# Wider sums, another order of x units, a later operand sum and an earlier transpose in a fused attention and mixer kernel

## The chip, the cores and the metric

The kernel runs on one core of a Trainium2 chip. The metric is the device time of one execution, in microseconds (us); the median of three runs stands for a kernel. One further execution is recorded by the profiler, and all durations below come from that one.

Engines are named as in the profile: PE is TensorE's matmuls and PEld its weight loads, DVE is VectorE, ACT is ScalarE, POOL is GpSimd, and SP is the queue that issues most DMA transfers. [...]

## The reference

Two stages follow each other, over 8 batches of 576 rows. The first is linear attention with 8 heads of 64 columns:

```
q_p, k_p = phi(q), phi(k)      # relu, times a cosine and a sine of the row: 64 -> 128 features
kv  = k_p^T v ;  z = sum of k_p over the rows
x   = (q_p kv) / (q_p z + 1e-06)
```

The second is a low-rank mixer over rows and a two-layer network over the 512 columns:

```
u   = x + ((x^T U) V)^T                 # U: 576 x 32, V: 32 x 576
out = u + relu(u w1) w2                 # w1: 512 x 2048, w2: 2048 x 512
```

Inputs and output are float32; the matmuls run in bfloat16.

## The kernel before

The 576 rows of a batch are held as four chunks of 128 rows (c = 0 to 3) and a tail of 64 rows (c = 4); two batches' tails share one tile. The order on each engine is the order in which the program is written: nothing is rescheduled. The program is a list of **slots**, each a piece of PE work that is large (one `g1` unit of four 128x512 matmuls into `g_ps`, or a quarter of an output tile, `g2_part`, four matmuls into `o_ps`, or an eighth part of a Strassen-like product, `half_part`, eight 128x256 matmuls into `h_ps`). Between the slots hang smaller pieces, keyed by slot number: `at(j, ...)` for batch 1, `attention_plan` with the table `PLAN` for batches 2 to 7, and `put` for operand sums and stores. Each piece runs behind the slot with its number. So attention of the next batch is woven into the network of the one before, and PE always has a slot to go on with.

The parts that the change touches:

- **Batch 0's start** (`first_chain`, from L1119). PE sums k over the rows: for each chunk and head one matmul with a column of ones (`v_tl[:, 0, D:E]`) as its moving operand, into one column of `z_ps` (L1207), with one 128x512 matmul on zeros per chunk for nothing but PE's activity (L1212). ACT copies the 8 columns to `z_sb` (L126). `den_mm` (L1053) then forms the denominators `d_ps`: two matmuls write the constant 1e-06, in two parts, and 20 matmuls with one column of `z_sb` each add to it; DVE takes the reciprocal (L1130, L1141). `z_ps`, `d_ps` and the later x units use the one two-bank tile X, so each waits until the one before it is emptied.
- **Batch 1's x units** (slots 15 to 24). `kv_unit` twice (bank T, emptied by DVE), then one x unit per chunk. `x_unit` (L418) writes eight matmuls into X; DVE adds 1e-06 to the denominators, takes the reciprocal and multiplies (L408, L409, L428). `x_two` (L1268) writes four heads to bank T and four to a bank called `side`, with a reciprocal each, and for batch 1 ACT multiplies all eight heads, one 128x64 product at a time (L1278). The order is unit 0 (`x_two`) and 4 behind slot 18, 1 and 2 (`x_two`) behind 20, 3 behind 21. `A_unit` behind slot 23 (bank T) needs all five, `u_mm` and four `u_add` follow behind 24, and DMA transposes turn u into `uT` (L514), which batch 1's first `g1` reads at slot 32.
- **Operand sums** (`hid_sum`, L818). Each half of a Strassen-like product needs four sums over `hid`. The fourth is issued inside `half_part`, right behind the second product, ahead of whatever hangs behind that slot. Its reader is the product with number 3.
- **Batch 5's q transposes** (`PLAN[5]`). After the q features, three DMA transposes on SP bring q into the layout that the x units read: the tail (`q_tlT`, L392) and two halves (`q_pT`, L387). The table's third tuple gives their slots relative to 127: the tail at 113, the halves at 120 and 122. Between them SP issues two `uT` transposes of batch 4 (slots 117 and 119) and the query load of batch 6 (slot 119). SP issues strictly in order, and `q_pT` has one buffer, free when batch 4's last x unit (slot 112) has read it.

Of the kernel before, what the change touches and what calls it, by code (L numbers as in the profile page):

```python
# [17 lines left out]
def kernel(  # L18
# [22 lines left out]
    NJ = DH // P  # L41
    NPAIR = B // 2
    TS = 64
    EPS = (9.98377799987793e-07, 1.622538547962904e-09, 1.0)

    def tail(b):
# [171 lines left out]
    V_.memset(v_ext[:, 0:4, :, D:E], 1.0)  # L218
    V_.memset(q_tlT, 0.0)
    V_.memset(x_tl, 0.0)  # L220
    eps = pool.tile([1, 2 * P + 20], BF16, tag="S2", bufs=2, name="eps")
    for cs, part in zip((slice(0, P), slice(P, 2 * P), slice(2 * P, None)), EPS):
        V_.memset(eps[:, cs], part)

    def keep_warm(n, tag, bufs, short=0, cols=P):
# [103 lines left out]

    def k_of(b, c, h):  # L330
        return k_p[b][:, c, h, :] if c < 4 else k_tl[:, h, :]

    z_sb = const.tile([P, H], BF16)

    def kv_unit(b, hg, tag, bufs, eng=None, n=E):
        if b not in kv_sb:
# [481 lines left out]
        eng.tensor_tensor(out=o, in0=x, in1=y, op=op)  # L818

    ring, turn = ["o0", "o1"], [0]  # L820
    halves = {}

    def bank(i):
# [20 lines left out]
    def half_part(b, n, k, form):  # L844


        c2 = n + 2
        i = ORDER[form][k]
        if k == 0:
            halves[b, n] = {  # L850
                "o": [
                    pool.tile([P, DM], FP32, tag="o_sb", bufs=8, name="o_sb") for _ in range(2)
                ]
            }
            if form == "alone":
                halves[b, n]["s"] = pool.tile([P, DM], FP32, tag="o_sb", bufs=8, name="s_sb")
        w = halves[b, n]
        s1, s2 = hid_s.get((b, n, 1)), hid_s.get((b, n, 2))
        to, lhs, rhs = {
            1: ("X", h_of(b, 0, n), W2[0]),  # L860
            2: ("Y", h_of(b, 1, n), W2[2]),
            3: ("Z", h_of(b, 1, n), W2[3]),
            4: ("X" if form == "with g" else "Q", h_of(b, 1, c2), w2_s[3]),
            5: ("Z", s1, w2_s[0]),
            6: ("X", s2, w2_s[1]),
            7: ("X", h_of(b, 0, c2), w2_s[2]),
        }[i]
        at = BANKS[form].get(i)
        if at is not None:
            w[to] = bank(at)  # L870
        acc = w[to][:, 0:256]
        for j in range(8):
            nc.tensor.matmul(  # L873
                out=acc, lhsT=lhs[:, j, :], rhs=rhs[:, j, :],
                start=(j == 0 and at is not None), stop=(j == 7),
                skip_group_check=at is None,
            )
        lo, hi = slice(0, 256), slice(256, 512)
        o, o2 = w["o"]
        u = [[u_of(b, c, g) for g in range(2)] for c in (n, c2)]  # L880

        def first(t, cs, c, g):
            add(V_, by_n(t[:, cs]), u[c][g], by_n(acc))

        def more(t, cs):
            add(V_, t[:, cs], t[:, cs], acc)

        if form == "alone":
            ss = w["s"]
            if i == 1:  # L890
                cast(A_, ss[:, lo], acc)
            elif i == 2:
                first(o, lo, 0, 0)
            elif i == 5:
                cast(A_, o2[:, hi], acc)
            elif i == 6:
                cast(A_, ss[:, hi], acc)
            elif i == 4:
                cast(A_, o2[:, lo], acc)
                add(G_, by_n(o2), by_n(o2), u_bf[b][:, :, c2, :])  # L900
            elif i == 3:
                first(o, hi, 0, 1)
                add(G_, o, o, ss)
            elif i == 7:
                o2v = o2.rearrange("p (g n) -> p g n", g=2)
                add(V_, o2v, o2v, acc.unsqueeze(1).to_broadcast([P, 2, 256]))
        elif i == 1:
            first(o, lo, 0, 0)
        elif i == 2:
            more(o, lo)  # L910
        elif i == 6:
            first(o, hi, 0, 1)
        elif i == 5:
            first(o2, hi, 1, 1)
        elif i == 3:
            more(o, hi)
        elif i == 4:
            first(o2, lo, 1, 0)
        else:
            if form == "last":  # L920
                more(o2, lo)
            more(o2, hi)
        if i == 2:
            hid_sum(b, n, 4)
        if k == 6:
            turn[0] += 1

# [35 lines left out]
    def spare(at):  # L963
# [9 lines left out]
        2: (46, -15, V_, V_, -10, (-5, -4, -4)),  # L973
        3: (64, -12, V_, A_, -7, (3, 3, 18)),
        4: (100, (-20, 1, V_, V_), (-13, 2, A_, V_), -12, (-9, -4, -4)),
        5: (127, (-24, 2, A_, A_), (-14, 2, A_, V_), (-14, -7, -5), (-8, -4, -4)),
        6: (157, (-24, 2, A_, A_), (-14, 2, A_, V_), (-14, -8, -6), (-8, -4, -4)),
        7: (191, (-24, 2, A_, A_), (-14, 2, A_, V_), (-14, -12, -10), ()),
    }
# [73 lines left out]
    def den_mm(b, h0, h1, d_ps):  # L1053
        for i in range(2):
            nc.tensor.matmul(
                out=d_ps.rearrange("p c h -> p (c h)"), lhsT=eps[:, i * P : i * P + P],
                rhs=eps[:, 2 * P :], start=(i == 0), stop=(i == 1),
            )
        for c in range(5):
            for h in range(h0, h1):  # L1060
                nc.tensor.matmul(
                    out=d_ps[:, c, h - h0 : h - h0 + 1],
                    lhsT=qT_of(b, c, h),
                    rhs=z_sb[:, h : h + 1],
                    start=False,
                    stop=True,
                    skip_group_check=True,
                )
# [50 lines left out]
    def first_chain(b):  # L1119
# [4 lines left out]
        cast(V_, kv_sb[b][:, 0:4, 0:D], kv_lo)  # L1124
        spread_evac(A_)
        d0 = ps.tile([P, 2, 512], FP32, tag="X", bufs=1, name="d_ps")
        d = [d0[:, i, 0:20].rearrange("p (c h) -> p c h", h=4) for i in range(2)]
        rec = [pool.tile([P, 5, 4], FP32, tag="rec5", bufs=2, name="rec5") for _ in (0, 1)]
        den_mm(b, 0, 4, d[0])
        V_.reciprocal(out=rec[0], in_=d[0])  # L1130
        x0 = [xh_mm(b, c, 0, *G3) for c in ORD[0:3]]
        for n in (0, 1):
            xh_norm(b, ORD[n], 0, rec[0], x0[n])
# [4 lines left out]
        xh_scale(b, ORD[3], 0, rec[0], x0[3])  # L1138
        xh_norm(b, ORD[2], 0, rec[0], x0[2])
        xh_norm(b, ORD[4], 0, rec[0], x0[4])  # L1140
        V_.reciprocal(out=rec[1], in_=d[1])  # L1141
        x1 = [xh_mm(b, c, 4, *G3) for c in ORD[0:2]]
        a_ps = ps.tile([P, DM], FP32, tag="o", bufs=2, name="a_ps")
        x1.append(xh_mm(b, ORD[2], 4, *G3))
# [53 lines left out]
    cast_u()  # L1198
    spread_v()
    z_all = ps.tile([P, 2, 512], FP32, tag="X", bufs=1, name="z_ps")  # L1200
    z_ps = z_all[:, 0, 0:H]
    kv_sb[0] = pool.tile([P, H, E], BF16, tag="kv", bufs=2, name="kv")
    kv_lo = ps.tile([P, 4, D], FP32, tag="T", bufs=1, name="kv_ps")
    for c in TL:
        k_prep(0, c, FEATS[c])
        for h in range(H):
            nc.tensor.matmul(  # L1207
                out=z_ps[:, h : h + 1], lhsT=k_of(0, c, h), rhs=v_tl[:, 0, D:E],
                start=(c == 0 and h == 0), stop=(c == 4 and h == H - 1),
            )  # L1210
        if c < 4:
            nc.tensor.matmul(  # L1212
                out=z_all[:, 1, :], lhsT=zero[:, 0:P], rhs=zero, start=True, stop=True
            )
# [35 lines left out]
        for i in range(2):  # L1250
            at((14, 15)[i], lambda c=c, i=i: v_prep(1, 4 * i, 4 * i + 4, (c,), (V_,)))
    for hg in range(2):
        at((15, 17)[hg], lambda hg=hg: kv_unit(1, hg, "T", 1))

    side = {}

    def x_two(b, c, *hi):
        x_alloc(b)
        rows = slice(0, P) if c < 4 else tail(b)
        if not hi and not side:  # L1260
            side["g"] = ps.tile([P, 512], FP32, tag="g", bufs=3, name="side")
        lo = ps.tile([P, 512], FP32, tag="T", bufs=1, name="x2_ps")
        up = ps.tile([P, 512], FP32, tag=hi[0], bufs=hi[1], name="x2_ps") if hi else side["g"]
        accs = [
            t[:, 0 : 4 * E].rearrange("p (i e) -> p i e", e=E) for t in (lo, up)
        ]
        for h in range(H):
            nc.tensor.matmul(  # L1268
                out=accs[h // 4][:, h % 4, :], lhsT=qT_of(b, c, h), rhs=kv_sb[b][:, h, :],
                start=(h % 4 == 0), stop=(h % 4 == 3),  # L1270
            )
        rec = pool.tile([P, 2, 4], FP32, tag="rec", bufs=2, name="rec")
        n = P if c < 4 else TS
        for g, acc in enumerate(accs):
            recip(rec[rows, g, :], acc[rows, :, D])
            if b in (1, 3):
                for i in range(4):
                    nc.scalar.activation(  # L1278
                        out=x_of(b, c)[:, (4 * g + i) * D : (4 * g + i + 1) * D],
                        in_=acc[:, i, 0:D], func=AF.Copy, bias=0.0,  # L1280
                        scale=rec[:, g, i : i + 1],
                    )
                continue
            nc.vector.tensor_tensor(
                out=x_of(b, c, rows)[:, g * 256 : g * 256 + 256].rearrange(
                    "p (i d) -> p i d", d=D
                ),
                in0=acc[rows, :, 0:D],
                in1=rec[rows, g, :].unsqueeze(2).to_broadcast([n, 4, D]),
                op=ALU.mult,  # L1290
            )

    for a, c in ((18, 0), (18, 4), (20, 1), (20, 2), (21, 3)):
        if c in (0, 2):
            at(a, lambda c=c: x_two(1, c))
        else:
# [156 lines left out]
        put(n, lambda n=n: [store() for store in late[n]])  # L1453
    for i, s in enumerate(slots):
        s()
        for t in todo.get(i, []):
            t()


# [28 lines left out]
```

## Time and profile before

| | |
|---|---|
| runs | 295.67, 295.90, 296.99 us; median 295.9 |
| profiled execution | 295.29 us, its span 293.5 us |
| PE busy | 283.6 us (97%), 2878 matmuls |
| DVE busy | 208.1 us (71%) |
| ACT busy | 160.3 us (55%) |
| POOL busy | 53.9 us (18%) |
| granted TensorE clock | 1.0 over the span |
| DMA | 54.07 MB, mean 184 GB/s |

The span runs from the first to the last instruction; 1.8 us of the execution's time lie outside it. The page of the profile lists busy times, the chain of work that ended last (followed back from the last instruction to whatever released each step), and groups of instructions. A group's line gives engine, operation, output and inputs, shapes, count, and mean time. The timeline lists instructions in order of time, with the idle time before one and what ended it in brackets. The view of waits lists who waited for whom, in total, how often, and the longest. A line such as L418 is a line of the kernel's file; many pieces share a helper's line.

### The profile page before, as it was taken

Reading aid. Unit: us, or ns where it says so; the run is one execution under the profiler, and the core shown is the slowest. Engines: PE = TensorE matmul, PEld = TensorE weight load, DVE = VectorE, ACT = ScalarE, POOL = GpSimd, SP = SyncE. Lnnn points to the kernel's source line nnn. Section 1 sums busy time; section 2 is a strip of 40 time slices with the busy share of each in tenths; the row PEclk is TensorE's granted clock in tenths of the full one; section 3 lists DMA queues with packets and bytes.
Section 4 is the critical chain, followed back from the end, with each engine's and each line's share of the span. In section 5 each row is a group of like instructions: output and inputs, shape, how many; then the busy total and the mean of one; then the engine's idle time right before and its main releaser. Section 6 shows DMA issues by size and latency. Waiting matters only on the chain.

```text
span 293.5 us, 7181 instructions
## 1 busy us (share of the span) xinstructions
PE 283.6 (97%) x2878; PEld 191.4 (65%) x2915; DVE 208.1 (71%) x500; ACT 160.3 (55%) x321; POOL 53.9 (18%) x89
## 2 busy tenths in 40 slices
PE   7799999999999999999999999999999999999995
PEld 4584554446645545676757666766877668889884
DVE  4976845777875579947746794678747788785864
ACT  2955744075791867478735865378752334446220
POOL 8520400012020002410500261022200100000240
PEclk9999999999999999999999999999999999999999
DMA  6999999999997878999689939992900141101013
GB/s 210 291 251 250 283 181 183 247 311 210 323 209 195 271 202 216 233 315 308 133 193 229 296 92 246 250 318 66 250 3 3 74 89 75 71 2 71 2 73 145
DMA packets 90709, 54.07 MB, mean 184 GB/s; under 512 B 58420, under 2 KB 87380, under 8 KB 90676
## 3 DMA queue, kind: packets, MB, share of 16 engines
q1 hardware_dynamic: 84116, 43.85, 59.5%
q0 software_dynamic: 6416, 9.63, 14.9%
q8 instruction: 23, 0.38, 0.5%
q10 hardware_dynamic: 144, 0.13, 0.1%
q14 instruction: 10, 0.08, 0.1%
HBM read 36.86 MB, written 9.44 MB: 158 GB/s over the span
## 4 chain that ended last, share of the span: by engine, by line
PE 86%; DMA 8%; DVE 2%; ACT 1%; issue 1%; SPq 0%; ACTq 0%; DVEq 0%
PE g_ps L572 31%; PE h_ps L873 26%; PE o_ps L744 10%; DMA qst<-in_q_dram 8%; PE gt_ps L706 5%; PE c_ps L666 4%; PE kv_ps L343 3%; PE x_ps L418 3%; PE h_ps L744 1%; PE a_ps L441 1%; PE t_ps L361 1%; PE va_ps L471 1%; ACT q_p L302 1%; DVE x_bf L428 0%; PE va_ps L492 0%
## 5 line engine op out<-in xcount | busy, mean ns | idle before, releaser
L581 ACT ACTIVATE hid<-g_ps 128x512 bf16<-128x512 f32 x112 | 66.2, 598 | 73.5 <-PE g_ps L572 73.2
L572 PE MATMUL g_ps<-uT,w_bf 128*128 128x512 bf16 x413 | 105.0, 379 | 1.3
L572 PEld LDWEIGHTS <-w_bf 128*128 128x128 bf16 x440 | 41.4, 98 | 37.3 <-issue 0.2
L873 PEld LDWEIGHTS <-hid 128*128 128x128 bf16 x480 | 45.4, 98 | 10.0 <-issue 0.5
L873 PE MATMUL h_ps<-w_bf,hid 128*128 128x256 bf16 x288 | 37.1, 273 | 0.0
L128 POOL CAST v_ext<-vst 128x512 bf16<-128x512 f32 (+1 forms) x26 | 21.1, 836 | 57.7 <-DMA vst<-in_v_dram 49.3
L831 DVE TENSOR_TENSOR o_sb<-u_bf,h_ps 128x256 f32<-128x256 bf16 x44 | 18.3, 416 | 18.1 <-PE h_ps L873 17.9
L744 PE MATMUL o_ps<-w_bf,hid 128*128 128x512 bf16 x122 | 29.5, 379 | 0.3
L873 PE MATMUL h_ps<-w_s,S 128*128 128x256 bf16 x208 | 26.5, 272 | 0.0
L873 PE MATMUL h_ps<-w_s,hid 128*128 128x256 bf16 x192 | 24.9, 273 | 0.2 <-DVE o_sb L831 0.2
L931 POOL DMA_DIRECT2D out_dram<-o_sb x16 | 10.0, 625 | 80.2 <-DVE o_sb L831 78.8
L479 DVE TENSOR_TENSOR u_bf<-x_bf,va_ps 128x512 bf16<-128x512 bf16 x27 | 17.7, 680 | 7.9 <-PE va_ps L471 5.5
L873 PEld LDWEIGHTS <-S 128*128 128x128 bf16 x208 | 20.0, 98 | 4.3
L831 DVE TENSOR_TENSOR o_sb<-o_sb,h_ps 128x256 f32<-128x256 f32 (+1 forms) x36 | 15.4, 431 | 10.2 <-PE h_ps L873 9.9
L744 PEld LDWEIGHTS <-hid 128*128 128x128 bf16 x128 | 11.5, 98 | 12.2
L706 PE MATMUL gt_ps<-uT_tl,w_bf 128*128 128x128 bf16 x256 | 16.1, 219 | 0.0
L428 DVE TENSOR_TENSOR x_bf<-x_ps,rec 128x512 bf16<-128x512 f32 x22 | 15.2, 691 | 0.8
L706 PEld LDWEIGHTS <-w_bf 128*128 128x128 bf16 x256 | 15.0, 98 | 1.0
L302 ACT ACTIVATE k_p<-kst,cosw 128x512 bf16<-128x512 f32 x20 | 14.2, 713 | 0.1
L302 ACT ACTIVATE q_p<-qst,sinw 128x512 bf16<-128x512 f32 x18 | 12.6, 709 | 2.4 <-DMA qst<-in_q_dram 2.4
L604 DVE TENSOR_TENSOR hid<-kept,c_ps 128x256 bf16<-128x256 f32 x24 | 9.5, 418 | 5.3 <-PE c_ps L666 2.8
L304 DVE TENSOR_SCALAR k_p<-kst,sinw 128x512 bf16<-128x512 f32 x24 | 13.1, 549 | 0.0
(188 smaller groups left out, 409.1 us busy)
## 6 DMA issues: line engine op xcount, KB each, us to landing
qst<-in_q_dram SPq DMA_DIRECT2D x14, 512.0 KB, 6.0
kst<-in_k_dram SPq DMA_DIRECT2D x14, 512.0 KB, 6.9
vst<-in_v_dram SPq DMA_DIRECT2D x12, 512.0 KB, 7.2
out_dram<-o_sb POOLq DMA_DIRECT2D x19, 256.0 KB, 3.8
w_bf<-in_moe_w_ch_dram POOLq DMA_DIRECT2D x8, 512.0 KB, 11.5
out_dram<-o_sb SPq DMA_DIRECT2D x16, 256.0 KB, 2.7
qst<-in_q_dram SPq DMA_DIRECT2D x2, 640.0 KB, 13.7
kst<-in_k_dram SPq DMA_DIRECT2D x2, 640.0 KB, 8.4
```

What stands on the lines that cost most here:

```text
L128: eng.tensor_copy(out=o, in_=i)
L302: nc.scalar.activation(out=o, in_=i, func=AF.Relu, bias=0.0, scale=w)
L304: eng.tensor_scalar(out=o, in0=i, scalar1=0.0, scalar2=w, op0=ALU.max, op1=ALU.mult)
L428: nc.vector.tensor_tensor(out=x_of(b, c, rows).rearrange("p (g i d) -> p g i d", g=2, d=D), in0=view[:, :, :, 0:D], in1=rec[rows].unsqueez ...
L479: nc.vector.tensor_tensor(out=u_bf[b][:, j, :, :], in0=x_bf[b][:, :, ns], in1=va[b][j].rearrange("p (c n) -> p c n", c=4), op=ALU.add,)
L572: nc.tensor.matmul(out=g_ps.rearrange("p (c t) -> p c t", c=4), lhsT=w1_bf[:, d, j * P : j * P + P], rhs=uT[b][:, d, :, :], start=(d == 0) ...
L581: nc.scalar.activation(out=hid[b][:, j, :], in_=g_ps, func=AF.Relu, bias=0.0, scale=1.0)
L666: nc.tensor.matmul(out=w[to].rearrange("p (c t) -> p c t", c=2), lhsT=lhs[:, d, cs], rhs=rhs[:, d], start=(first and d == 0), stop=(d == 1 ...
L706: nc.tensor.matmul(out=g_ps[:, jj, :], lhsT=w1_bf[:, d, j * P : j * P + P], rhs=uT_tl[pr][:, d, :], start=(d == 0), stop=(d == 3),)
L744: nc.tensor.matmul(out=o[:, cols], lhsT=lhs[:, j, c * P : c * P + P], rhs=w2_bf[:, j, cols], start=(j == 0), stop=(j == NJ - 1),)
L831: eng.tensor_tensor(out=o, in0=x, in1=y, op=ALU.add)
L873: nc.tensor.matmul(out=acc, lhsT=lhs[:, j, :], rhs=rhs[:, j, :], start=(j == 0 and at is not None), stop=(j == 7), skip_group_check=at is ...
```

## The change

Four edits. The sums of k and the denominators are computed over 24 equal columns (`NZ`): z is kept 24 times per head, in the tile `eps`, and only column 0 of each denominator is read. Batch 1's second `kv_unit` goes from slot 17 to 16, the x units run in the order 4, 0, 1, 3, 2, and of each `x_two` of batch 1 the second four heads are multiplied by DVE in one 128x256 product (as batch 2 does), the first four by ACT as before. The fourth operand sum is put on a list and issued behind what hangs at its slot. Batch 5's first `q_pT` transpose goes from slot 120 to 113.

```diff
+    NZ = 24
...
-    eps = pool.tile([1, 2 * P + 20], BF16, tag="S2", bufs=2, name="eps")
-    for cs, part in zip((slice(0, P), slice(P, 2 * P), slice(2 * P, None)), EPS):
+    eps = pool.tile([P, 2 * P + 24 + H * NZ], BF16, tag="S2", bufs=2, name="eps")
+    z_sb = eps[:, 2 * P + 24 :].rearrange("p (h n) -> p h n", n=NZ)
+    for cs, part in zip((slice(0, P), slice(P, 2 * P), slice(2 * P, 2 * P + 24)), EPS):
         V_.memset(eps[:, cs], part)
...
-    z_sb = const.tile([P, H], BF16)
...
+    behind = []
...
         if i == 2:
-            hid_sum(b, n, 4)
+            behind.append(lambda: hid_sum(b, n, 4))
...
-        5: (127, (-24, 2, A_, A_), (-14, 2, A_, V_), (-14, -7, -5), (-8, -4, -4)),
+        5: (127, (-24, 2, A_, A_), (-14, 2, A_, V_), (-14, -14, -5), (-8, -4, -4)),
...
             nc.tensor.matmul(
-                out=d_ps.rearrange("p c h -> p (c h)"), lhsT=eps[:, i * P : i * P + P],
-                rhs=eps[:, 2 * P :], start=(i == 0), stop=(i == 1),
+                out=d_ps[:, :, :, 0], lhsT=eps[0:1, i * P : i * P + P],
+                rhs=eps[0:1, 2 * P : 2 * P + 20], start=(i == 0), stop=(i == 1),
             )
...
-                    out=d_ps[:, c, h - h0 : h - h0 + 1],
+                    out=d_ps[:, c, h - h0, :],
                     lhsT=qT_of(b, c, h),
-                    rhs=z_sb[:, h : h + 1],
+                    rhs=z_sb[:, h, :],
...
-        V_.reciprocal(out=rec[0], in_=d[0])
+        V_.reciprocal(out=rec[0], in_=d[0][:, :, :, 0])
...
-                out=z_ps[:, h : h + 1], lhsT=k_of(0, c, h), rhs=v_tl[:, 0, D:E],
+                out=z_ps[:, h, :], lhsT=k_of(0, c, h), rhs=eps[:, 2 * P : 2 * P + NZ],
...
-        at((15, 17)[hg], lambda hg=hg: kv_unit(1, hg, "T", 1))
+        at((15, 16)[hg], lambda hg=hg: kv_unit(1, hg, "T", 1))
...
-            if b in (1, 3):
+            if b == 3 or (b, g) == (1, 0):
...
-    for a, c in ((18, 0), (18, 4), (20, 1), (20, 2), (21, 3)):
+    for a, c in ((18, 4), (18, 0), (19, 1), (20, 3), (21, 2)):
         if c in (0, 2):
             at(a, lambda c=c: x_two(1, c))
         else:
             at(a, lambda c=c: x_unit(1, c, "X", 1))
...
         s()
-        for t in todo.get(i, []):
+        for t in todo.get(i, []) + behind:
             t()
+        behind.clear()
```

More of the change, by code (lines that the diff above doesn't have):

```diff
@@ L1126, in first_chain @@
         d0 = ps.tile([P, 2, 512], FP32, tag="X", bufs=1, name="d_ps")
-        d = [d0[:, i, 0:20].rearrange("p (c h) -> p c h", h=4) for i in range(2)]
+        d = [
+            d0[:, i, 0 : 20 * NZ].rearrange("p (c h n) -> p c h n", h=4, n=NZ) for i in range(2)
+        ]
         rec = [pool.tile([P, 5, 4], FP32, tag="rec5", bufs=2, name="rec5") for _ in (0, 1)]
         den_mm(b, 0, 4, d[0])
-        V_.reciprocal(out=rec[0], in_=d[0])
+        V_.reciprocal(out=rec[0], in_=d[0][:, :, :, 0])
         x0 = [xh_mm(b, c, 0, *G3) for c in ORD[0:3]]
@@ L1140, in first_chain @@
         xh_norm(b, ORD[4], 0, rec[0], x0[4])
-        V_.reciprocal(out=rec[1], in_=d[1])
+        V_.reciprocal(out=rec[1], in_=d[1][:, :, :, 0])
         x1 = [xh_mm(b, c, 4, *G3) for c in ORD[0:2]]
@@ L1200 @@
     z_all = ps.tile([P, 2, 512], FP32, tag="X", bufs=1, name="z_ps")
-    z_ps = z_all[:, 0, 0:H]
+    z_ps = z_all[:, 0, 0 : H * NZ].rearrange("p (h n) -> p h n", n=NZ)
     kv_sb[0] = pool.tile([P, H, E], BF16, tag="kv", bufs=2, name="kv")
```

## The prediction

> **What bounds the kernel now.** I read the page first. The chain that ended last says who carries the end:
>
> ```profile
> PE 86%; DMA 8%; DVE 2%; ACT 1%; issue 1%; SPq 0%; ACTq 0%; DVEq 0%
> ```
>
> TensorE (PE) is busy for 283.6 of the 293.5 us, and DVE, at 71%, for 208.1. So an edit counts only where it moves a wait of PE, or PE's own work. Next I read PE's waits, and those of its weight loads (PEld), over the whole span. The columns are total, times, longest. Behind the first 25 us only two causes are left that this change touches:
>
> ```profile
> PE x_ps L418 <- DVE x_bf L428: 0.3, 2, 0.2
> ```
>
> ```profile
> PEld L418 <- DMA q_pT<-q_p: 0.3, 1, 0.3
> ```
>
> The two waits on `x_bf` lie at 46.2 us (batch 1) and 132.8 us (batch 4). The weight load that waits for `q_pT` is batch 5's, at 158.08 us; its matmul still started where the one before it ended, so here it cost nothing, with no room to spare. PE's records overlap (a matmul of 0.38 us starts every 0.216), so I take stalls from starts. PE around the first wait:
>
> ```profile
> 44.63 0.42 PE L418 MATMUL x_ps<-kv,q_pT 128*128 128x65 bf16 x8
> ...
> 45.15 1.02 PE L744 MATMUL o_ps<-w_bf,hid 128*128 128x512 bf16 x4
> 46.35 0.43 PE L418 MATMUL x_ps<-kv,q_pT 128*128 128x65 bf16 x8 [0.17 <-DVE x_bf L428]
> ```
>
> Four `o_ps` matmuls take 4 x 0.216 = 0.865 us, so 46.35 should have been 45.15 + 0.865 = 46.01: a stall of 0.34 us. Both L418 units write the one X tile, and the second must wait until DVE has emptied the first. DVE's timeline shows that chain, and behind it what one `x_two` asks of DVE:
>
> ```profile
> 45.09 0.17 DVE L408 TENSOR_SCALAR rec<-x_ps 128x8 f32<-128x8 f32 x1 [0.58 <-PE x_ps L418]
> 45.29 0.20 DVE L409 RECIPROCAL rec<-rec 128x8 f32<-128x8 f32 x1
> 45.60 0.69 DVE L428 TENSOR_TENSOR x_bf<-x_ps,rec 128x512 bf16<-128x512 f32 x1
> 46.20 0.15 DVE L408 TENSOR_SCALAR rec<-x_ps 128x4 f32<-128x4 f32 x1
> 46.39 0.18 DVE L409 RECIPROCAL rec<-rec 128x4 f32<-128x4 f32 x1
> 46.49 0.13 DVE L408 TENSOR_SCALAR rec<-side 128x4 f32<-128x4 f32 x1
> 46.65 0.18 DVE L409 RECIPROCAL rec<-rec 128x4 f32<-128x4 f32 x1
> ```
>
> From the unit's first matmul (44.63) to the next use of X (46.35) is 1.72 us with DVE free; from 45.09 to the end of the product at 46.29 is 1.20.
>
> **Sums over 24 columns.** The count of matmuls and weight loads stays: 40 for `z_ps`, 40 for `d_ps`. What one costs is its distance to the next. The trace has one column and 64:
>
> ```profile
> 15.32 0.34 PE L1207 MATMUL z_ps<-v_tl,k_tl 128*128 128x1 bf16 x8
> 15.53 0.63 PE L1107 MATMUL kv_ps<-v,k_p 128*128 128x64 bf16 x16
> ```
>
> (0.34 - 0.163) / 7 = 25 ns and (0.63 - 0.193) / 15 = 29 ns, so 24 columns lie between: 0 to 80 x 4 = 0.3 us, nearest to one column; I take +0.1. [...] The copy of z on ACT grows from 8 columns (0.18 us) towards 256 (0.40): about +0.17. `z_sb` ended at 15.88 and the first `d_ps` matmul, which waits for it, started at 16.20 behind `kv_ps` matmuls, so these hide it; uncovered it would be 0.17 at most. Behind it in ACT's queue stand the copies of `V_bf` and `V_tl`, and then 1.53 us of idle time. The wider memsets have the same length per partition. Below nothing: timed runs that lose time here, and the profiled one does not, would gain (rivals).
>
> **Batch 1's units.** By the order of the built program PE now runs: first `kv_unit`, one `o_ps` slot, second `kv_unit`, two slots, unit 4 and unit 0, a slot, unit 1, a slot, unit 3, a slot, unit 2, two slots, `A_unit`. Up to unit 4 nothing waits: the first `kv` copy ended at 39.82, and the second unit wants its bank at 38.59 + 0.60 + 0.865 = 40.06. Unit 4 starts at 42.39 as unit 0 did. From there by hand:
>
> - Unit 1 wants X at 42.39 + 0.26 + 0.26 + 0.865 = 43.78 and gets it at 42.39 + 1.72 = 44.11: stall 0.33.
> - DVE ends unit 4's product 1.66 after its start, at 44.05. Then unit 0: its four small steps by the rows above, plus the product over 128x256 that the change brings from ACT to DVE (0.42, row L1284): in all 0.99 behind the product before it, 45.04. Unit 1's chain starts 0.08 before that and takes 1.20: 46.16, and PE follows 0.06 later, at 46.22. Unit 3 wanted X at 44.11 + 0.26 + 0.865 = 45.24: stall 0.98.
> - Unit 2 follows at 47.34. DVE has unit 3 until 47.88, then unit 2's steps; ACT's four products end at about 49.17. `A_unit` wants that bank at 49.33: no stall, with 0.16 to spare.
>
> So 1.31 us of stall replaces 0.34: +0.97. Taking four products off ACT saves nothing, since nothing waits for ACT there. One thing is given back: at 56.48 PE waited 0.12 for `uT` of batch 1, landed 3.8 to 4.4 us after issue beside the query loads, where later ones take 2.7; all of that shifts with PE while the loads do not, so I take -0.12. Bounds: 0.5, if DVE's small steps overlap more than in the rows; 1.6, if they do not overlap at all (0.2 more in each of two units) and `A_unit` then waits as well.
>
> **Fourth operand sum behind attention.** DVE at the second wait:
>
> ```profile
> 131.21 0.69 DVE L818 TENSOR_TENSOR hid<-hid,S 128x1024 bf16<-128x1024 bf16 x1
> 131.81 0.16 DVE L408 TENSOR_SCALAR rec<-x_ps 128x8 f32<-128x8 f32 x1
> ...
> 132.24 0.69 DVE L428 TENSOR_TENSOR x_bf<-x_ps,rec 128x512 bf16<-128x512 f32 x1
> ```
>
> Now the L818 sum goes behind the product, so X is free 0.6 us earlier, at 132.33 and not 132.94. PE wanted it at 131.79 + 0.87 = 132.66 and got it at 132.99: the stall of 0.33 goes, -0.33. The sum's reader, cross product 3, comes four products and as many `g1` units later (some 7 us). What comes next on DVE is the add at 132.87, in place as before. In later batches the sum trades places with one `u_add`, where PE waits for neither; in the last half batches it goes behind the first sum of the next half, and PE shows no gap there: nothing.
>
> **Batch 5's first q transpose** moves from slot 120 to 113 and on SP ahead of two `uT` transposes and the query load:
>
> ```profile
> 134.24 2.88 SPq L392 DMA_TRANSPOSE q_tlT<-q_tl  x1
> 143.07 3.16 SPq L514 DMA_TRANSPOSE uT<-u_bf  x2
> ...
> 149.16 8.18 SPq L387 DMA_TRANSPOSE q_pT<-q_p  x2
> ```
>
> It waits for batch 4's last x unit (137.2) and batch 5's q features (133.8), so it issues at about 137.3 in an empty stretch of SP; even the longest issue of such a transpose (5.15 us) ends before 143.07. Landings took 3.7 to 8.9 us; the free stretch suggests 4, some 15 us before its reader. `uT` is not delayed. Cost 0; gain 0 in this execution, but without it the 0.33 of batch 4 would be lost again at 158.08. Timed runs in which that landing came later than here gain more: I take -0.2 for the median, between 0 and -0.6.
>
> **The sum.** +0.1 + 0.97 - 0.12 - 0.33 + 0 = +0.62 on the profiled execution, 295.29 to 295.9. The median of the runs, 295.9, stands 0.61 above it: 296.5, less 0.2 for the q transpose, is **296.3 us**. What can be told from no change is about 0.5%, 1.48 us: below 294.4 is faster, above 297.4 slower.
>
> **Rivals.**
>
> - *The X tile becomes a longer chain, and A waits too* (slower, 0.2). Place: 42 to 50 us. DVE's five steps of `x_two` run end to end, as two different PSUM readers side by side suggest (ACT's 128x64 products stretch from 305 to 357 ns there), unit 2 ends 0.4 later, and past 0.16 of that `A_unit` waits. The upper bound of 1.6, the sums at +0.3 and nothing won in batch 4: 295.9 + 1.9 = 297.8. For it: two units one slot apart need 1.72 and have 1.13. Against it: the rows overlap.
> - *The X chain costs half* (0.18): 0.5 us, with the transpose at -0.6: 295.9 + 0.1 + 0.5 - 0.12 - 0.33 - 0.6 = 295.4. For it: the highest run, 296.99, shows that 1.7 us can be lost somewhere that the profile does not lose it.
> - *The sums were what cost time in the timed runs* (faster, 0.09). If the clock drops behind the one-column stretch (13.35 to 16.85), 3.5 us of PE run at a 512-column distance of 0.427 (the first rows of the trace) in place of 0.216: 1.7 us, the highest run's distance. 24 columns would end it: with X at 0.5, 295.9 - 1.7 + 0.5 - 0.12 - 0.33 = 294.2. Against it: the granted clock is 1.0 all along, and 128x512 matmuls take 376 to 379 ns from 11 us on. [...]
> - *It does nothing*: sums bound by weight loads, the transpose early for nobody. That is in the forecast.
>
> **The numbers.** Forecast 0.53, own range 295.8 to 297.0. Faster 0.09 (the third rival), slower 0.23 (the first rival and 0.03 of the forecast), within 0.5% 0.68 (the rest). The range, 294.8 to 297.8, leaves out the third rival and about half of the first.
>
> **What would show it.** After: PE gaps of about 0.3 and 1.0 us ahead of units 1 and 3 between 43 and 47 us, both released by DVE L428; `A_unit` some 1.0 later; no x wait near 133; `q_pT` issued near 138. Wrong if those two gaps are missing, if PE waits for `uT` of batch 4, or if `z_ps` matmuls stand further apart than 30 ns.

## The result and the profile after

The kernel after takes 297.53 us (median of 22 runs, 295.6 to 302.21); the kernel before, run beside it, 295.69 us (22 runs). The ratio is 1.0059 with a 95% interval of [1.0034, 1.0085]: 1.7 us slower, 1.0 to 2.5. The forecast of 296.3 us is 1.2 us too low, outside its own range of 295.8 to 297.0 and inside the wide one of 294.8 to 297.8; the loss is just past the 0.5% that the prediction called no change. All ratios leave out executions over 1.5% above the fastest of their kernel, and since the profiled ones of `e4_columns` and `e5_before_shift` below were among these, only landings, packet times and PE's start are read from those two profiles.

The profiled execution after took 298.32 us, its span 296.4: 3.0 us more than before. These lines answer to those shown of before. First the chain that ended last, then PE's waits on X and on transposes (total, times, longest):

```profile
PE 80%; DVE 8%; DMA 6%; POOL 3%; issue 2%; SPq 1%; ACT 0%; DVEq 0%; POOLq 0%
```

```profile
PE g_ps L572 <- DMA uT<-u_bf: 1.4, 2, 1.1
...
PE x_ps L418 <- DVE x_bf L428: 0.9, 1, 0.9
```

PE is on the chain for six points less, and a wait of PE stands there that the prediction did not have: g1 units waiting for `uT`. PE and DVE in batch 1, from the timeline:

```profile
44.93 0.43 PE L418 MATMUL x_ps<-kv,q_pT 128*128 128x65 bf16 x8
...
45.20 1.02 PE L744 MATMUL o_ps<-w_bf,hid 128*128 128x512 bf16 x4
...
46.41 0.69 DVE L428 TENSOR_TENSOR x_bf<-x_ps,rec 128x512 bf16<-128x512 f32 x1
...
47.16 0.43 PE L418 MATMUL x_ps<-kv,q_pT 128*128 128x65 bf16 x8 [0.94 <-DVE x_bf L428]
```

Unit 3 starts at 47.16 where 45.20 + 0.865 = 46.07 was possible: a stall of 1.10. From starts in the same way, unit 1 (44.93) lost 0.27. Then batch 1's first g1 unit, again PE's timeline. Before, its four matmuls ran in one piece, after a short wait:

```profile
56.27 1.14 PE L572 MATMUL g_ps<-uT,w_bf 128*128 128x512 bf16 x4
```

After:

```profile
58.20 0.59 PE L572 MATMUL g_ps<-uT,w_bf 128*128 128x512 bf16 x2
59.85 0.59 PE L572 MATMUL g_ps<-uT,w_bf 128*128 128x512 bf16 x2 [1.06 <-DMA uT<-u_bf]
```

Two matmuls, then 1.22 us (by starts) until the second half of `uT` has landed. At batch 4 DVE has the product ahead of the fourth operand sum, as intended, and PE no longer waits for X:

```profile
134.68 0.69 DVE L428 TENSOR_TENSOR x_bf<-x_ps,rec 128x512 bf16<-128x512 f32 x1
135.29 0.68 DVE L818 TENSOR_TENSOR hid<-hid,S 128x1024 bf16<-128x1024 bf16 x1
135.70 0.42 PE L418 MATMUL x_ps<-kv,q_pT 128*128 128x65 bf16 x8
```

The SP queue around the moved transpose:

```profile
138.04 2.59 SPq L392 DMA_TRANSPOSE q_tlT<-q_tl  x1
140.75 5.52 SPq L387 DMA_TRANSPOSE q_pT<-q_p  x1
146.36 3.04 SPq L514 DMA_TRANSPOSE uT<-u_bf  x2
```

Both `uT` halves landed 5.7 us after issue (2.7 and 4.1 before), and PE lost 0.49 (152.40 + 2 x 0.216 = 152.83 to 153.32):

```profile
152.40 0.59 PE L572 MATMUL g_ps<-uT,w_bf 128*128 128x512 bf16 x2
153.32 1.02 PE L572 MATMUL g_ps<-uT,w_bf 128*128 128x512 bf16 x4 [0.32 <-DMA uT<-u_bf]
```

So batch 1 costs 1.03 for X and 1.1 more for `uT`, batch 4 gives 0.33 and loses 0.49. Another 0.9 is there ahead of all of that: the first g1 unit of the kernel starts at 23.42 us, before at 22.53. These parts add up to 3.2 us, 0.2 more than the two executions differ by. `z_ps` matmuls are not the cause of the 0.9:

```profile
15.06 0.35 PE L1210 MATMUL z_ps<-eps,k_p 128*128 128x24 bf16 x8
```

(0.35 - 0.173) / 7 = 25 ns, as with one column. But the granted clock (the PEclk column, behind the busy times of PE, PEld, DVE, ACT and POOL) was a half for 3.4 us, so that it is 0.993 over the span:

```profile
7.00:8.00 1.00, 0.00 (x0) 0.00 (x0) 0.00 (x0) 0.00 (x0) 1.00 (x2) 1.00 1.11 328
8.00:9.00 1.00, 0.00 (x0) 0.00 (x0) 0.84 (x2) 0.86 (x2) 1.00 (x3) 0.99 1.09 328
9.00:10.00 1.00, 0.88 (x9) 0.91 (x10) 1.00 (x3) 1.00 (x3) 1.00 (x3) 0.50 1.08 363
10.00:11.00 1.00, 1.00 (x13) 1.00 (x10) 1.00 (x4) 0.70 (x2) 1.00 (x2) 0.50 1.08 355
```

That belongs to this execution: below, kernels that keep one column show such a window too (8.6 to 12.0 us in `e2_transpose`), and 16 of the 22 timed executions of the kernel after have 0.998 or more over the span.

One line that the prediction had no eye for separates the two kernels best, the median time from issue to landing in the list of DMA issues. Before:

```profile
uT<-u_bf SPq DMA_TRANSPOSE x14, 2.7
```

After:

```profile
uT<-u_bf SPq DMA_TRANSPOSE x14, 3.2
```

### The profile page after: what moved, and what is told of

Same layout as the page of the kernel before. It is cut to its first block, busy times and chain, and to the rows that moved or that the text cites. A ratio compares the mean times of both kernels' runs of the same rounds, so it can differ in the third digit from the quotient of the medians.

```text
span 296.4 us, 7208 instructions
## 1 busy us (share of the span) xinstructions
PE 286.8 (97%) x2915; PEld 193.3 (65%) x2915; DVE 209.0 (70%) x502; ACT 159.1 (54%) x313; POOL 50.7 (17%) x89
## 4 chain that ended last, share of the span: by engine, by line
PE 80%; DVE 8%; DMA 6%; POOL 3%; issue 2%; SPq 1%; ACT 0%; DVEq 0%; POOLq 0%
PE h_ps L874 26%; PE g_ps L572 25%; PE o_ps L744 8%; PE c_ps L666 4%; PE gt_ps L706 4%; DMA uT<-u_bf 3%; PE kv_ps L343 3%; DMA qst<-in_q_dram 3%; PE x_ps L418 2%; PE t_ps L373 1%; DVE u_bf L479 1%; DVE q_p L306 1%; PE a_ps L441 1%; DVE w_s L789 1%; DVE k_p L306 1%
## 5 line engine op out<-in xcount | busy, mean ns | idle before, releaser
L572 PE MATMUL g_ps<-uT,w_bf 128*128 128x512 bf16 x440 | 107.3, 379 | 1.4 <-DMA uT<-u_bf 1.4
L744 PE MATMUL o_ps<-w_bf,hid 128*128 128x512 bf16 x128 | 30.3, 379 | 0.0
L129 POOL CAST v_ext<-vst 128x512 bf16<-128x512 f32 (+1 forms) x26 | 17.8, 709 | 61.9 <-DMA vst<-in_v_dram 60.9
L874 PE MATMUL h_ps<-w_s,hid 128*128 128x256 bf16 x192 | 24.9, 272 | 0.2 <-DVE o_sb L832 0.2
```

The source lines that it names most:

```text
L129: eng.tensor_copy(out=o, in_=i)
L572: nc.tensor.matmul(out=g_ps.rearrange("p (c t) -> p c t", c=4), lhsT=w1_bf[:, d, j * P : j * P + P], rhs=uT[b][:, d, :, :], start=(d == 0) ...
L744: nc.tensor.matmul(out=o[:, cols], lhsT=lhs[:, j, c * P : c * P + P], rhs=w2_bf[:, j, cols], start=(j == 0), stop=(j == NJ - 1),)
L874: nc.tensor.matmul(out=acc, lhsT=lhs[:, j, :], rhs=rhs[:, j, :], start=(j == 0 and at is not None), stop=(j == 7), skip_group_check=at is ...
```

## The experiments

Each group of four ran on one chip beside the kernel before, so ratios are to be compared rather than medians. Packet times are means over the trace's records of 55,296 packets of 256 bytes (mostly the transposes) and 25,600 of 1024 bytes (the loads, mostly); they include the few packets that took over 200 ns (in the kernel before, 291 of the former and 272 of the latter).

**One edit at a time**, each on the kernel before.

```diff
# e1_units: second kv_unit, units, products of batch 1
-        at((15, 17)[hg], ...
+        at((15, 16)[hg], ...
-            if b in (1, 3):
+            if b == 3 or (b, g) == (1, 0):
-    for a, c in ((18, 0), (18, 4), (20, 1), (20, 2), (21, 3)):
+    for a, c in ((18, 4), (18, 0), (19, 1), (20, 3), (21, 2)):
```

> The kernel before with batch 1's part alone: second kv_unit at slot 16, units in the order 4, 0, 1, 3, 2, DVE multiplying the second four heads. Own sum of the prediction: two X stalls of 0.3 and 1.0 us in place of 0.34, and uT of batch 1 not later: +1.0 us. Late transposes (read from the profile after): the same stalls, and besides them PE waits 1.1 us for the second uT half of batch 1, because SP's first transpose there takes 2.3 us to issue in place of 1.3: +2.1. Chance (that uT wait belongs to one execution and not to the edit): stalls of X alone in this profile, +1.0 in the times.

Ratio 1.0050 [1.0008, 1.0093], 0.2 to 2.7 us. The profile has stalls of 0.27 and 1.10 for X and no wait for `uT`. The size of the X chain was right; in this execution the units by themselves did not make `uT` late.

```diff
# e2_transpose
-        5: (..., (-14, -7, -5), (-8, -4, -4)),
+        5: (..., (-14, -14, -5), (-8, -4, -4)),
```

> The kernel before with batch 5's first q transpose at slot 113 alone. Own sum: q_pT issues near 138 and ends before uT of batch 4 is ready, no wait: 0 to -0.3. Late transposes: q_pT's issue takes over 5 us, its packets lie ahead of uT's, both uT halves of batch 4 land some 5.7 us after issue and not 2.7 to 4.1, and PE waits 0.3 to 0.6 us near 150: +0.5. Chance: landings of 3 to 4 us and no wait.

Ratio 1.0003 [0.9961, 1.0045], and no wait for `uT` of batch 4. Nor did the early transpose by itself make it late in this execution.

```diff
# e3_sum
         if i == 2:
-            hid_sum(b, n, 4)
+            behind.append(lambda: hid_sum(b, n, 4))
```

> The kernel before with the fourth operand sum behind attention alone. Both theories: the x wait of 0.33 us near 133 goes and nothing else moves: -0.3 us. Rival: the sum, now later, is what a product waits for, or the two places where PE waits 0.3 to 0.4 us for DVE ahead of h_ps products (120.8 and 244) grow: 0 to +0.5.

Ratio 0.9993 [0.9950, 1.0036]: 0.3 us is below what the times can tell. In the profile the x wait near 133 is gone and no product waits for the sum.

```diff
# e4_columns: z, its copy and the denominators over NZ columns, as in the change
-    z_sb = const.tile([P, H], BF16)
+    z_sb = eps[:, 2 * P + 24 :].rearrange("p (h n) -> p h n", n=NZ)
...
```

> The kernel before with z and the denominators over 24 columns alone. Own sum: z_ps and d_ps matmuls 25 to 29 ns apart as before, copy hidden: +0.1, 0 to +0.3. Rival (the start): the profile after showed the granted clock at a half from 9.0 to 12.4 us and its first g1 unit 1.1 us later; if the wider sums or their tile cause that, +1.1 and such a window here too. If that window is chance, the clock is at a half in some executions of both kernels and this edit costs 0 to 0.3.

Ratio 1.0096 [1.0052, 1.0139]: 2.8 us, from the edit that was priced at 0.1. No theory on record had that. Its `uT` landed after 3.2 us (median of 14) against 2.7 in the other three, and packets of 256 bytes took 25.0 ns (21.4 to 23.3 in the others), those of 1024 bytes 65.0 (60.1 to 61.4). The granted clock is not what differs: over the executions with 0.998 or more, `e4_columns` averages 298.0 us (7) and the kernel before on that chip 295.2 (21). The edit changes no DMA. What it also does is to take `z_sb` out of the constants: 16 bytes a partition in a slot of 32. In the built program every tile behind it moves down by 32 bytes. Before, `qst`, `kst` and `vst` start at bytes 83200, 93440 and 103680 of a partition, 325, 365 and 405 times 256, and `q_p`, `q_pT`, `u_bf` and `uT` lie on multiples of 256 too; after, all of them lie 32 bytes below one.

**The address.** The next four put that to the test.

```diff
# e5_before_shift: the kernel before, one more constant behind z_sb
     z_sb = const.tile([P, H], BF16)
+    pad = const.tile([P, H], BF16)
+    V_.memset(pad, 0.0)
```

> The kernel before with one more constant of 16 bytes a partition (a slot of 32) behind z_sb, so that every tile allocated behind it, the landing tiles of q, k and v and all tiles of the rotating pool, lies 32 bytes further; before it these lie on multiples of 64 bytes, now 32 past one. Nothing else changes but one memset of a few columns. New theory (address): taking z_sb out moved the same tiles by 32 bytes the other way, which slows DMA packets of 256 and 1024 bytes (means 21 to 23 and 60 to 61 ns in the kernels with z_sb, 25 to 26 and 64 to 65 in the two without), and this is the whole cost of the columns: the same packet means here and +2 to +3 us. Rival (the columns themselves, or their place in a tile of the pool): no change, packet means as before.

Ratio 1.0078 [1.0036, 1.0120], 2.3 us, packets at 25.3 and 65.3 ns, and `uT`:

```profile
uT<-u_bf SPq DMA_TRANSPOSE x14, 3.3
```

Nothing but addresses has changed, and a memset of 8 columns at the start, which the next two kernels have as well without this loss. Over the executions with a granted clock of 0.998 or more, it averages 297.2 us (7) and the kernel before 295.5 (25). So the address alone costs it.

```diff
# e6_after_pad: the kernel after; e7_columns_pad: e4 with the same two lines
+    pad = const.tile([P, H], BF16)
+    V_.memset(pad, 0.0)
```

> The kernel after with an unused constant in the place of z_sb, so that all tiles behind it lie as before the change. Address: packets as in the kernel before, no wait for uT of batch 1 or of batch 4; what is left is X at +1.0, the sum at -0.3 and the columns at 0 to 0.3: +0.7 us against before, about 1 us faster than after. Rival (late transposes come from the units and from the early q_pT): the waits of 1.1 and 0.5 us stay, +1.7 as after.

Ratio 1.0022 [0.9987, 1.0057], 0.65 us at its middle where 0.7 was expected. The waits of PE on X stay and those on `uT` are gone; PE's view of waits and timeline:

```profile
PE x_ps L421 <- DVE x_bf L431: 0.9, 1, 0.9
```

```profile
57.80 1.46 PE L747 MATMUL o_ps<-w_bf,hid 128*128 128x512 bf16 x6
59.17 1.02 PE L575 MATMUL g_ps<-uT,w_bf 128*128 128x512 bf16 x4
60.12 0.26 PE L495 MATMUL va_ps<-A_sb,V_tl 32*64 32x128 bf16 x8
```

```profile
uT<-u_bf SPq DMA_TRANSPOSE x14, 2.7
```

The g1 unit that was cut in two by 1.22 us now runs in one piece. The interval overlaps that of the kernel after, so by times alone the gain of 1.1 us is not settled; by the profile it is two waits less.

> The kernel before with z and the denominators over 24 columns, and an unused constant in the place of z_sb. Address: the +2.8 us of the columns alone goes to the 0 to 0.3 of the prediction. Rival: it stays above +2.

Ratio 1.0003 [0.9981, 1.0025], against 1.0096 [1.0052, 1.0139] without the pad: the intervals are far apart. The 24 columns cost nothing that can be measured; where they were put cost 2.7 us. Packets are back at 23.2 and 61.4 ns.

> The kernel before with the units, the sum behind attention and the early q transpose, sums over one column and z_sb as before. Address: like the padded kernel, X +1.0 and sum -0.3: +0.7 us, no uT wait. Rival (late transposes come from units and early q_pT): +1.7, with PE waits for uT near 57 and near 150.

(The edits of e1, e2 and e3 together.) Ratio 1.0012 [0.9976, 1.0049], no wait for `uT` near 57 or 150, X stalls of 0.27 and 1.10.

**Which offset, which tiles.**

```diff
# e9_shift128: as e5, but
+    pad = const.tile([P, 64], BF16)
# e10_shift_landing: as e5, and behind qst, kst, vst
+    gap = pool.tile([P, 112], BF16, tag="gap", bufs=1, name="gap")
# e11_shift_rest: no pad, only
+    gap = pool.tile([P, 16], BF16, tag="gap", bufs=1, name="gap")
```

> The kernel before with 128 bytes more in front of the same tiles: their addresses, multiples of 256 before, now lie 128 past one. Theory 256 (a 256-byte packet that starts off a multiple of 256 bytes costs more): packets of 256 bytes near 25 ns and +2 us, as with 32 bytes. Theory 64 (only the offset within 64 or 128 bytes counts): packets as before, 22 to 23 and 60 to 61 ns, and no change in time.

Packets of 256 and 1024 bytes took 24.9 and 63.6 ns, and `uT` landed after 3.3 us, as with 32 bytes: for the packets, a multiple of 128 is not enough. The time, 1.0026 [0.9992, 1.0059], is less than the +2 us that the first theory gave, and does not exclude no change.

> The kernel before with only the landing tiles of q, k and v (qst, kst, vst) moved by 32 bytes; the tiles behind them lie 256 bytes further, at the same offset within 256 as before. If the loads carry the cost: 1024-byte packets at 64 to 65 ns, 256-byte ones (mostly the transposes) near 23, and most of +2.3 us. If the transposes do: packets as before and no change.

Packets of 1024 bytes at 64.9 ns, those of 256 at 23.2, `uT` after 2.8 us: packets of loads slower, transposes as before. Ratio 1.0014 [0.9984, 1.0044], not to be told from no change. Its profile shows one new wait, at batch 5's second x unit, where the prediction saw no room to spare; that the slower loads cause it is not shown:

```profile
159.42 0.43 PE L422 MATMUL x_ps<-kv,q_pT 128*128 128x65 bf16 x8 [0.36 <-DMA q_pT<-q_p]
```

> The kernel before with the landing tiles in place and all tiles of the rotating pool behind them, those that the transposes read and write among them (q_p, q_pT, u_bf, uT), moved by 32 bytes. If the transposes carry the cost: 256-byte packets near 25 ns, 1024-byte ones near 61, and most of +2.3 us. If the loads do: packets as before and no change.

The reverse: packets of 256 bytes at 24.3 ns, of 1024 at 60.2, `uT`:

```profile
uT<-u_bf SPq DMA_TRANSPOSE x14, 3.2
```

Ratio 0.9998 [0.9957, 1.0040]. So each packet size slows with the tiles that it touches, and neither group alone shows the 2.3 us that both expectations gave to one of them. How the loss is shared, and whether it grows when both are slow, stays open: the intervals are 0.6 to 0.8% wide. Open too is through which waits the slower packets cost PE its 2 to 3 us: in the profiles of `e9_shift128` and `e11_shift_rest` `uT` landed late and no wait of PE for it is listed.

**A version of its own.**

```diff
# e12_spread: e2 and e3, z_sb in place, e1's kv slot and products, but the units one slot apart
-    for a, c in ((18, 0), (18, 4), (20, 1), (20, 2), (21, 3)):
+    for a, c in ((17, 4), (18, 0), (19, 1), (20, 2), (21, 3)):
```

> A version that should beat both: the kernel before with z_sb and one column kept, the sum behind attention, the early q transpose, the second kv_unit at slot 16, and the units one slot apart, 4, 0, 1, 2, 3 behind 17 to 21, so that two users of X are two slots apart: 0.87 + 0.26 + 0.87 + 0.26 = 2.25 us against the 1.72 that X needs. Own sum: no x wait at batch 1 (-0.34) nor at batch 4 (-0.33), -0.7 us against before. Rival (DVE, which has about 2.2 us of unit work for each 2.25 us of PE there, falls behind, or the first unit waits for the kv copy): stalls of 0.1 to 0.5 us stay between 41 and 48 us, and the gain is -0.2 to -0.5.

Median 295.08 us against 296.10 for the kernel before on that chip, ratio 0.9970 [0.9937, 1.0002]; the kernel after stands at 1.0059 [1.0034, 1.0085]. It is faster than the kernel after; its lead on the kernel before is likely and not quite shown. PE and DVE in batch 1:

```profile
43.47 0.42 PE L418 MATMUL x_ps<-kv,q_pT 128*128 128x65 bf16 x8
...
44.37 0.69 DVE L428 TENSOR_TENSOR x_bf<-x_ps,rec 128x512 bf16<-128x512 f32 x1
...
44.85 1.02 PE L744 MATMUL o_ps<-w_bf,hid 128*128 128x512 bf16 x4
...
45.71 0.42 PE L418 MATMUL x_ps<-kv,q_pT 128*128 128x65 bf16 x8
```

Unit 3 starts at 44.85 + 0.865 = 45.71, without a gap; the product that frees X had ended at 45.06. The two units that use X start 2.24 us apart. This kernel too waits 0.2 us for `uT` of batch 1, at 56.39 us.

## Why the prediction was right and wrong, step by step

- **What bounds the kernel**: right. Every loss that was traced to a place is a wait of PE, or PE at half its clock.
- **Sums over 24 columns, +0.1**: right for what it priced (matmuls 25 ns apart; `e7_columns_pad` at 1.0003), and the step that failed. It went through matmuls, copy and memsets and named `z_sb` only as the copy's target. That the tile leaves the constants, and what lies behind it, was not asked, and the bounds of 0 to 0.3 had no room for the 2.8 us of `e4_columns`. That 297.5 still lies in the wide range is luck: the upper end, 297.8, was worked out for the first rival, which did not happen.
- **Batch 1's units, +0.97**: right. Stalls of 0.33 and 0.98 were worked out; 0.27 and 1.10 came, in all four kernels that have the edit, so +1.03. `A_unit` did not wait.
- **-0.12 at `uT` of batch 1**: 1.2 us came in its place in the profile after, and nothing in `e1_units`, `e6_after_pad` and `e8_no_columns`; `e3_sum`, `e7_columns_pad` and `e12_spread` list 0.2 there. The reason given, loads that do not shift with PE, was no good guide: the first transpose took 2.28 us to issue and the second half landed 3.9 us behind its own issue.
- **Fourth operand sum, -0.33**: right in the profile, too small for the times.
- **Early q transpose, 0**: right where tiles lie on multiples of 256. In the profile after PE did wait for `uT` of batch 4 (0.49 us), which the prediction had named as a sign of being wrong. There its issue took 5.52 us and ended at 146.27, right where the `uT` issues began, and these landed late; in `e6_after_pad` it took 4.73, they landed after 4.0 us, and PE did not wait. The 0.2 for timed runs is not visible in `e2_transpose`. The wait it guards against came in `e10_shift_landing` (0.36 us). That may be why the address costs 2.8 us beside the columns alone and some 1.1 in the whole change; this is argued from single profiles, not shown, and the intervals do not exclude that both costs are equal.
- **Rivals.** The first came nearest in number (297.8), by a mechanism that did not happen: DVE's steps did not run longer (0.17, 0.20 and 0.69 us in unit 3, as in the unit shown before; 0.15, 0.18, 0.13 and 0.18 in unit 2, within 0.01 us as far apart as in the `x_two` shown before) and `A_unit` did not wait (its first matmul, at 50.37, lists no wait). The second failed on its 0.5 for X. The third, a clock that the one-column stretch lowers, is not borne out: a half-clock window comes with 24 columns (after, 9.0 to 12.4 us) and with one (`e2_transpose`, 8.6 to 12.0), both times behind PE's idle time at the start, and the change did not make the kernel faster.

The means of the packets of 256 bytes go with the start addresses of the transposes' tiles: 21.4 to 23.4 ns on multiples of 256, 24.3 to 25.8 at 32 below or past one and at 128 past one. But the median packet of 256 bytes took 18 ns in every run; the share that took over 19 ns grew from 4 to 6% to 14 to 15%, and in the kernel after 1.5 of the 3.1 ns by which the mean grew come from packets over 200 ns, 342 in place of 291. Why some packets are slowed there and most are not is not shown. Transposes of tiles off a multiple of 256 by 32 or 128 bytes landed 0.5 to 0.6 us later (3.2 to 3.3 us after issue in place of 2.7).

## What to carry to other kernels

Ask of each tile that an edit adds, removes or resizes what is allocated behind it, and compare the start addresses of all tiles that a DMA reads or writes before and after; here the place of one constant of 16 bytes cost 2 to 3 us. Compare the landing times of equal transfers in the two profiles early: a median over 14 transposes told the two kinds of kernel apart in every profiled execution, where times needed dozens of runs. It points at the tiles and does not give the cost: `e11_shift_rest` landed late and lost no time that can be measured. Before two users of one PSUM tile (here X, which PE writes and DVE empties) are moved closer, add up what frees it (here 1.72 us) and keep at least that much PE work between them.

## What the runs showed of the hardware

- The offset of a tile within 256 bytes changes the mean time of its DMA packets: at 32 or 128 bytes off, packets of 256 bytes took 24.3 to 25.8 ns in place of 21.4 to 23.4, of 1024 bytes 63.6 to 65.3 in place of 60.1 to 61.4, and transposes of `u_bf` landed after 3.2 to 3.3 us in place of 2.7 (2.8 in one). The plain loads of 512 KB did not land later by their medians (q 6.0 us before and 5.8 after, k 6.9 in both, v 7.2 in both). With all of these tiles 32 bytes off (`e5_before_shift`) it cost the kernel 2.3 us in 296; 128 bytes off (`e9_shift128`, ratio 1.0026 [0.9992, 1.0059]), no loss of time is shown.
- The granted clock dropped to a half for 3.41 us (after, 9.0 to 12.4 us; as long in `e2_transpose`, 8.6 to 12.0) behind waits of PE at the start. Where PE's idle time ahead of the first transposes, as the timeline gives it, was 2.18 us or less (the kernel before and seven experiments) no drop followed there; with 2.29 (after), 2.46 (`e2_transpose`) and 2.60 us (`e10_shift_landing`) one did. `e6_after_pad`, idle for 0.85 there, dropped at 16.4 us, behind a wait of 1.4 us for v. `e4_columns` dropped after 1.75 us of idle time and `e5_before_shift` did not after 2.34, so the length of the wait alone does not decide it. Nor does the number of columns: all twelve executions of `e7_columns_pad`, which has 24, kept 0.998 or more. On the chip of the last four experiments, executions of the kernel before with 0.993 or 0.994, which is about one such window, average 297.1 us (5), and those with 0.998 or more 295.2 (22).
